# Sixteen small matrix products at a time instead of thirty-two interleaved, with index tables and one transpose moved

## The chip, the cores and the metric

The kernel runs on one core of one Trainium2 chip. The metric is the time of one execution on the device, in microseconds. TensorE (PE in the profile, with PEld for its weight loads) multiplies, VectorE (DVE), ScalarE (ACT) and GpSimd (POOL) work on elements, and SyncE (SP) starts loads. Each engine takes its own instructions in the order of the program and waits for the others by semaphores.

## The reference

Three layers follow each other. An attention layer with a gated recurrent state (4 batches, 8 heads, 768 steps, head size 40) makes 3072 rows of 320 numbers:

```python
for t in range(S):
    m_new = np.maximum(f_gate[:, :, t] + m, i_gate[:, :, t])
    f_stab = np.exp(f_gate[:, :, t] + m - m_new)
    i_stab = np.exp(i_gate[:, :, t] - m_new)
    C = f_stab[...] * C + i_stab[...] * np.einsum('bhd,bhe->bhde', vt, kt)
    n = f_stab[...] * n + i_stab[...] * kt
    denom = np.maximum(np.abs(np.einsum('bhd,bhd->bh', n, qt)), 1.0)
    y[:, :, t] = sigmoid(o_gate[:, :, t]) * np.einsum('bhde,bhe->bhd', C, qt) / denom
```

Then every row goes to one of 8 experts, 384 rows to each, in the order of the gate's logits over all rows (`x @ w_gate`, greedy by value), and through that expert's two matrices (`relu(x @ w1[e]) @ w2[e]`). Last, a dense layer: `elu(x @ w_in) @ w_out` with 2048 hidden units.

## The kernel before

The attention is cut in 12 chunks of 64 time steps. A step `u` (24 of them, `NU`) is one chunk of two batches and 8 heads. In a chunk the recurrence is written as matrix products of 64x64 blocks, in fp32. Two batches lie at partitions 0 to 63 and 64 to 127, so each kind of product comes as 16 matmuls: head `h` of 8, half `r` of 2. Every such matmul uses one quarter (64 rows by 64 columns) of TensorE's array, and the profile lists two records for it. The four kinds of step `u` are

- `values(u)`: the weighted scores `P` times the values `VP`, into the output `pO`;
- `scores(u + 2)`: keys times queries, two steps ahead, into `pS`;
- `recall(u)`: the faded queries `qt` times the state `CS`, added to the same `pO`;
- `state(u)`: the faded keys `kt` times the values, into `pC`.

The halves of `values` and `recall` use the two quarters on one diagonal of the array, those of `scores` and `state` the two on the other. `both(...)` issues, head by head, one pair of every kind that it is given.

`run` sets the order of a step on every engine, and nothing reorders it afterwards. TensorE: `values` with `scores`, `recall` with `state`, the transposes of the step before (`turn(u - 1)`), the rows of decay factors (`decay(u + 2)`), the logits of the step before (`logits(u - 1)`). VectorE: `scan` (a scan that makes `W`), `weigh` (`P`), then the denominators (`gates`: `rd`), the sum of the state (`add_state`) and the output `x` (`rows_out`). GpSimd: `factors(u + 1)` (`vp`, `qt`), the output gate `sg` times the reciprocal, then `fade(u + 1)` (`kt` and the state's fading). Between these stand pieces of later stages: `fill()` converts a weight matrix, and `step()` works through generators in `extra`, the router's tables and first comparisons among them. The tables (`Router.tables`) are index patterns written by GpSimd (iota and memset), with a few VectorE instructions after them; they are started by `hook(2)`, after step 2.

`sel` is a matrix of zeros and ones (96 by 2048, bf16) that `decay` multiplies by; VectorE builds it from the small `i3` at the start. `turn` transposes `x` in three blocks of 128 columns: `x` has 320 columns, and ScalarE copies columns 256 to 319 once more to 320 to 383. `logits` takes 128, 128 and 64 rows of the transposed blocks.

After the attention comes the routing of the first expert, then the experts and the dense layer, in an order that a planner writes out while the program is built.

Of the kernel before, what the change touches and what calls it, by code (L numbers as in the profile page):

```python
# [12 lines left out]
AF = mybir.ActivationFunctionType  # L13
# [4 lines left out]
NS, NU = 12, 24  # L18
# [16 lines left out]
class Plan:  # L35
# [3 lines left out]
    def __init__(self):  # L39
        self.n = 0  # L40
        self.todo = []
        self.reset()
# [39 lines left out]
    def next(self):  # L82
        self.due(min(self.todo)[0])
# [30 lines left out]
class Attention:  # L114
# [1 line left out]

    def __init__(self, nc, tc, consts, qk, vk, ig, fg, wg, xd, L, ident):
        self.nc, self.tc, self.qk, self.vk, self.xd, self.L, self.ident = nc, tc, qk, vk, xd, L, ident  # L120
        self.es = ExitStack()
        one = self.es.enter_context(tc.tile_pool(name="a1", bufs=1))
        self.two = self.es.enter_context(tc.tile_pool(name="a2", bufs=2))
        self.psX = self.es.enter_context(tc.tile_pool(name="psX", bufs=1, space=PS))
        V, G, A = nc.vector, nc.gpsimd, nc.scalar
        self.st = {}
        self.extra = []
        gi = one.tile([32, S], F32, name="gi")
        gf = one.tile([32, S], F32, name="gf")
        nc.sync.dma_start(gf, fg)  # L130
        A.dma_start(gi, ig)
        junk = self.psum("pF", 1)
        wz = one.tile([128, 512], BF, name="wz")
        V.memset(wz, 0.0)

        def spin(n):

            for _ in range(n):
                nc.tensor.matmul(junk, wz[:, :128], wz, start=True, stop=True)

        spin(SPIN)
        warm = one.tile([1, 8], F32, name="warm")
        V.memset(warm, 0.0)
        A.activation(warm, warm, AF.Exp)
        self.QKb = [one.tile([128, 2, 2, 8, 64], F32, name=f"qk{i}") for i in range(3)]
        self.QK, self.VK, self.W = {}, {}, {}
        for bp in range(2):
            self.load_qk(0, bp)
        self.load_vk(0)
        self.load_qk(1)  # L150
        self.wg = one.tile([128, 3, 8], F32, name="wg")
        nc.sync.dma_start(self.wg, wg)
        self.load_vk(1)
        self.VP = [one.tile([128, 8, 64], F32, name=f"vp{i}") for i in range(2)]
        m = one.tile([32, S + 1], F32, name="m")
        V.memset(m[:, 0:1], -1e30)
        d1 = one.tile([32, S], F32, name="d1")
        G.memset(d1, 0.0)
        for x in self.VP:
            G.memset(x[:, :, 41:], 0.0)  # L160
        i3 = one.tile([96, 32], BF, name="i3")
        for k in range(3):
            V.tensor_copy(i3[k * 32:k * 32 + 32], ident[:32, :32])
        self.sel = one.tile([96, 16, 2, 64], BF, name="sel")
        V.tensor_copy(self.sel, i3.rearrange("p (r m) -> p m r", r=2)[:, :, :, None].to_broadcast([96, 16, 2, 64]))
        self.id8 = one.tile([128, 8, 64], BF, name="id8")
        for r in (0, 64):
            A.activation(self.id8[r:r + 64], ident[r:r + 64, None, r:r + 64].to_broadcast([64, 8, 64]), AF.Copy)
        self.fp = one.tile([96, S], BF, name="fp")
        self.CS = [[one.tile([128, 8, 64], F32, name=f"C{b}{i}") for i in range(3)] for b in range(2)]  # L170
        for x in self.CS[0] + self.CS[1]:
            G.memset(x[:, :, 41:], 0.0)
        self.dp = one.tile([96, S], BF, name="dp")
        self.isT = one.tile([128, NS, 16], F32, name="isT")
        self.pC = self.psum("pC", 1)
        self.pG = self.psum("pX", 1).rearrange("p h t -> p (h t)")
        self.g = gi, gf, m, d1

        t0, t1 = slice(0, 128), slice(128, S)
        self.maximum(0, 128)  # L180
        V.tensor_tensor(gf[:, t0], gf[:, t0], m[:, t0], op=ALU.add)
        V.tensor_tensor(gf[:, t0], gf[:, t0], m[:, 1:129], op=ALU.subtract)
        V.tensor_copy(d1[:, 64:65], gf[:, 64:65])
        V.memset(gf[:, 0:128:64], 0.0)
        V.tensor_tensor(gi[:, t0], gi[:, t0], m[:, 1:129], op=ALU.subtract)
        g0 = gf[:, t0].rearrange("p (s t) -> p s t", t=64)[:, :, 1:]
        A.activation(g0, g0, AF.Exp)
        A.activation(self.fp[:32, t0], gf[:, t0], AF.Copy)
        A.activation(gi[:, t0], gi[:, t0], AF.Exp)
        self.maximum(128, 128 + MX[0])  # L190
        for k in (1, 2):
            V.tensor_tensor(m[:, t0], (gf if k == 1 else m)[:, t0], self.fp[k * 32 - 32:k * 32, t0], op=ALU.subtract)
            A.activation(self.fp[k * 32:k * 32 + 32, t0], m[:, t0], AF.Copy)
            self.maximum(128 + MX[k - 1], 128 + MX[k])
        A.activation(d1[:, 64:65], d1[:, 64:65], AF.Exp)
        self.both(self.scores(0))
        self.turn_gi(0, 2)
        self.decay(0)
        self.keep_gi(0, 2)
        V.memset(self.pC, 0.0)  # L200
        V.tensor_tensor(gf[:, t1], gf[:, t1], m[:, t1], op=ALU.add)
        self.scan(0)
        V.tensor_tensor(gf[:, t1], gf[:, t1], m[:, 129:], op=ALU.subtract)
        A.activation(gf[:, t1], gf[:, t1], AF.Exp)
        self.decay(1)
        self.both(self.scores(1))
        self.factors(0)
        self.weigh(0)
        self.fade(0)
        V.tensor_tensor(gi[:, t1], gi[:, t1], m[:, 129:], op=ALU.subtract)  # L210
        A.activation(gi[:, t1], gi[:, t1], AF.Exp)
        self.products(1, 2)
        for _ in self.parts(self.dp, d1, slice(64, 128)):
            pass
        self.opens(0)
# [217 lines left out]

    def turn(self, u):
        x = self.st.pop(("x", u))
        p = self.st["T", u] = self.psum("pX", 1).rearrange("p h t -> p (h t)")
        for k in range(3):
            self.nc.tensor.transpose(p[:, k * 128:k * 128 + 128], x[:, k * 128:k * 128 + 128], self.ident)
        xT = self.st["xT", u] = self.two.tile([128, 3, 128], F32, name="xT")
        self.nc.scalar.activation(xT.rearrange("p k t -> p (k t)"), p[:, :384], AF.Copy)  # L440

    def logits(self, u):

        l = self.st.pop(("T", u))[:, 384:392]
        x = self.st.pop(("xT", u))
        for k in range(3):
            z = 128 if k < 2 else 64
            self.nc.tensor.matmul(l, x[:z, k], self.wg[:z, k], start=k == 0, stop=k == 2)  # L448
        self.nc.scalar.activation(self.L[:, :, u % 4 * 6 + u // 4], l, AF.Copy)

    def step(self):
# [4 lines left out]
    def run(self, hook, fill):  # L456
        later = self.later()
        for u in range(NU):
            v, w = u + 1, u + 2
            fl = lambda i: ([fill() for _ in range(FP[i])] if u > FU else []) + [self.step() for _ in range(EP[i])]  # L460
            if u % 2 == 0 and u // 2 + 2 < NS:
                self.load_qk(u // 2 + 2)
                self.load_vk(u // 2 + 2)
            self.both(self.values(u), self.scores(w))
            self.both(self.recall(u), self.state(u))
            if u > 0:
                self.turn(u - 1)
            if v < NU:
# [32 lines left out]
class Router:  # L501
# [9 lines left out]
    def tables(self):  # L511
        nc, c, stage = self.nc, self.c, self.stage
        G, V = nc.gpsimd, nc.vector
# [21 lines left out]
        d = stage.tile([128, 128], F32, name="tri0", bufs=1)  # L535
# [8 lines left out]
        self.ax = c.tile([128, 24], F32, name="ax")  # L544
        self.thr0 = stage.tile([128, 128], I32, name="thr0", bufs=1)
        m = stage.tile([128, 128], I32, name="tblt", bufs=1)
        V.tensor_scalar(jt, jt, 25, None, op0=ALU.logical_shift_left)
        yield
        V.tensor_scalar(m, jt, 31, -1, op0=ALU.arith_shift_right, op1=ALU.bitwise_xor)
# [853 lines left out]
def kernel(ctx, tc, qk, vk, ig, fg, wg, w1a, w1b, w2a, win, wout, out):  # L1403
    nc = tc.nc
    consts = ctx.enter_context(tc.tile_pool(name="c", bufs=1))
# [8 lines left out]
    plan = Plan()  # L1414
    m = Mlp(nc, tc, consts, w1a, w1b, w2a, win, wout, xd, out, ident, rt, plan)
    stage = ctx.enter_context(ExitStack())
    sp = stage.enter_context(tc.tile_pool(name="cv", bufs=2))
    at = Attention(nc, tc, consts, qk, vk, ig, fg, wg, xd, L, ident)

    wp = m.win_pieces(sp)  # L1420

# [3 lines left out]
    def hook(u):  # L1425
        if u == FU:
            fill()
            fill()
        if u == 2:
            rt.__init__(nc, tc, consts, wk, L, sp, plan)  # L1430
            at.extra.append(rt.tables())
            at.step()
        if 4 <= u < 23 and u % 4 == 0:
            at.extra.append(rt.early(u // 4 - 1))
        if u == 22:
            at.extra.append(rt.early(5, 0, 2))
        if u == 23:
            at.extra.append(rt.early(5, 2, 3))
        if u == 24:
            while at.extra:  # L1440
                at.step()
            rt.dg = rt.digits(0)
            for _ in rt.early(5, 3, 4, rt.dg):
                pass
# [18 lines left out]
def _layout(i):  # L1463
# [19 lines left out]
    d["vk"] = np.concatenate([a.reshape(12, 128, 2, -1) for a in (v, by_token(i["k"]), by_token(i["o_gate"])[:, ::-1])], 3)  # L1483
    d["ig"], d["fg"] = (i[n].reshape(2, 2, 8, 768).swapaxes(0, 1).reshape(32, 768) for n in ("i_gate", "f_gate"))
    wg = i["moe_w_gate"][:, ::-1]
    d["wg"] = np.concatenate([wg, np.zeros((64, 8), wg.dtype)]).reshape(3, 128, 8).transpose(1, 0, 2)
    d["w1a"] = i["moe_w1"][:, :256].reshape(2048, 1024)
    d["w1b"] = i["moe_w1"][:, 256:].reshape(512, 1024)
    d["w2a"] = i["moe_w2"].reshape(8, 2, 4, 128, 320).transpose(0, 1, 3, 2, 4).reshape(2048, 1280)
# [20 lines left out]
```

## Time and profile before

| | us |
|---|---|
| median of 3 runs | 819.77 (814.91 to 820.18) |
| the profiled execution | 817.59 |
| its span | 815.8 |
| attention, start to the first routing matmul | 0 to 166.5 |
| of it steps 3 to 22, first `values` to first `values` | 36.48 to 157.09 |
| routing of the first expert and start of the experts | 166.6 to 200 |
| experts and dense layer | 200 to 815.8 |

The span is what the profiler saw between the first and the last instruction; 1.8 us of the execution's own time lie around it. The profile is of one execution, and its own time stands 2.2 us under the median.

### The profile page before, as it was taken

How to read it: one execution, taken by the hardware profiler on the slowest of the kernel's cores; microseconds unless marked ns; L12 is line 12 of the kernel's file. 1: busy time of each engine (PE TensorE's matmuls, PEld its weight loads, DVE VectorE, ACT ScalarE, POOL GpSimd, SP SyncE). 2: the span in 40 equal slices, each digit the busy share in tenths (PEclk: the TensorE clock that was granted, in tenths of full speed). 3: DMA queues.
4: the chain of work that ended last, by engine and by line, in shares of the span. 5: the costliest groups of instructions: out<-in, count | busy, mean ns of one | idle time of the engine just before them, and what ended most of it. 6: DMA issues, size and time to landing. Idle time of an engine off the chain costs nothing.

```text
span 815.8 us, 18330 instructions
## 1 busy us (share of the span) xinstructions
PE 729.8 (89%) x7355; PEld 681.9 (84%) x7355; DVE 586.1 (72%) x1616; ACT 348.5 (43%) x743; POOL 309.2 (38%) x358
## 2 busy tenths in 40 slices
PE   7788788836899799799999999999999999999995
PEld 5678678725788789789989988898999999999995
DVE  8697878777979976987897679867733942862542
ACT  5343334324356533543553255325533633742431
POOL 3687887626425631633134125213410601201001
PEclk8678787856999999999999999999999999999998
DMA  8766855135114202112123103200500410100000
GB/s 343 253 216 209 278 186 187 43 107 199 54 30 139 83 27 78 51 44 100 32 65 93 40 0 106 67 27 0 172 12 13 138 35 25 65 1 26 1 1 25
DMA packets 20757, 72.79 MB, mean 89 GB/s; under 512 B 3200, under 2 KB 7296, under 8 KB 19264
## 3 DMA queue, kind: packets, MB, share of 16 engines
q1 hardware_dynamic: 8336, 35.08, 12.6%
q0 software_dynamic: 8448, 31.73, 11.8%
q10 hardware_dynamic: 3888, 4.82, 2.1%
q8 instruction: 58, 0.95, 0.5%
q14 instruction: 27, 0.22, 0.1%
HBM read 62.96 MB, written 8.65 MB: 88 GB/s over the span
## 4 chain that ended last, share of the span: by engine, by line
PE 58%; DVE 21%; issue 8%; ACT 4%; DMA 4%; POOL 2%; ACTq 1%; SPq 0%; POOLq 0%; DVEq 0%
PE ph L1096 24%; PE acc L1234 5%; PE acc L1238 4%; PE acc L1235 4%; PE acc L1203 3%; PE acc L1205 3%; PE acc L1204 3%; DVE e L1149 2%; DMA xd<-x 2%; PE pr L727 2%; DVE ge L713 1%; DVE gl L980 1%; PE acc L1190 1%; PE pX L448 1%; DMA vk<-in_vk_dram 1%
## 5 line engine op out<-in xcount | busy, mean ns | idle before, releaser
L1234 PE MATMUL acc<-woh,gh 128*128 128x320 f32 x384 | 122.7, 320 | 0.0
L1238 PE MATMUL acc<-woh,gl 128*128 128x320 f32 x384 | 119.7, 312 | 0.0
L1235 PE MATMUL acc<-wol,gh 128*128 128x320 f32 x384 | 119.0, 310 | 0.0
L1149 DVE SCALAR_TENSOR_TENSOR e<-e,ph 128x384 f32<-128x384 f32 x128 | 69.9, 549 | 61.8 <-ACT e L1146 61.4
L1145 ACT ACTIVATE e<-ph 128x384 f32<-128x384 f32 x128 | 62.7, 489 | 116.3 <-PE ph L1096 112.0
L980 POOL TENSOR_TENSOR gl<-e,gh 128x384 fp32r<-128x384 f32 x33 | 34.8, 1057 | 164.3 <-DVE gh L974 132.3
L1096 PE MATMUL ph<-yh,wih 128*128 128x384 f32 x256 | 89.7, 351 | 0.4
L1096 PE MATMUL ph<-yh,wil 128*128 128x384 f32 x256 | 86.2, 337 | 0.0
L1113 ACT ACTIVATE gh<-ph 128x384 fp32r<-128x384 f32 x64 | 31.3, 491 | 121.9 <-PE ph L1096 120.7
L1244 POOL DMA_INDIRECT out_dram<-ot,idx x24 | 24.0, 1001 | 141.3 <-ACT ot L972 138.1
L1120 DVE SCALAR_TENSOR_TENSOR gl<-ph,gh 128x384 fp32r<-128x384 f32 x64 | 35.4, 556 | 56.8 <-ACT gh L1113 56.4
L1238 PEld LDWEIGHTS acc<-woh,gl 128*128 128x128 f32 x384 | 72.5, 189 | 0.6
L1234 PEld LDWEIGHTS acc<-woh,gh 128*128 128x128 f32 x384 | 72.8, 190 | 0.2
L1235 PEld LDWEIGHTS acc<-wol,gh 128*128 128x128 f32 x384 | 72.7, 189 | 0.0
L1146 ACT ACTIVATE e<-e 128x384 f32<-128x384 f32 x128 | 67.3, 526 | 4.0
L1096 PE MATMUL ph<-yl,wih 128*128 128x384 f32 x256 | 66.5, 341 | 0.0
L980 DVE TENSOR_TENSOR gl<-e,gh 128x384 fp32r<-128x384 f32 x95 | 57.3, 607 | 1.9
L1096 PEld LDWEIGHTS ph<-yh,wih 128*128 128x128 f32 x256 | 48.4, 189 | 4.5 <-ACT yh L1208 4.4
L1096 PEld LDWEIGHTS ph<-yh,wil 128*128 128x128 f32 x256 | 48.3, 189 | 0.0
L1096 PEld LDWEIGHTS ph<-yl,wih 128*128 128x128 f32 x256 | 46.4, 189 | 0.0
L1096 PE MATMUL ph<-xh,w1h 128*128 128x384 f32 x128 | 45.0, 352 | 0.2
L1203 PE MATMUL acc<-gh,w 128*128 128x384 f32 x128 | 44.6, 349 | 0.0
(269 smaller groups left out, 2023.5 us busy)
## 6 DMA issues: line engine op xcount, KB each, us to landing
vk<-in_vk_dram SPq DMA_DIRECT2D x12, 968.0 KB, 8.7
qk<-in_qk_dram SPq DMA_DIRECT2D x11, 1024.0 KB, 8.0
wx<-in_wout_dram SPq DMA_DIRECT2D x16, 320.0 KB, 2.8
xd<-x ACTq DMA_DIRECT2D x48, 96.0 KB, 3.7
cx<-in_win_dram SPq DMA_DIRECT2D x8, 512.0 KB, 4.4
qk<-in_qk_dram SPq DMA_DIRECT2D x2, 512.0 KB, 5.9
cx<-in_win_dram SPq DMA_DIRECT2D x4, 256.0 KB, 4.2
xg<-xd,idx POOLq DMA_INDIRECT x24, 3.3
```

The source lines that it names most:

```text
L980: (self.nc.vector if e == "d" else self.nc.gpsimd).tensor_tensor(out, x, y, op=ALU.subtract)
L1096: PE.matmul(p, w, x, start=k == 0, stop=k == 7)
L1113: nc.scalar.activation(h, p, AF.Relu)
L1120: nc.vector.scalar_tensor_tensor(l, p, 0.0, h, op0=ALU.max, op1=ALU.subtract)
L1145: nc.scalar.activation(e, p, AF.Relu, scale=-1.0)
L1146: nc.scalar.activation(e, e, AF.Exp, scale=-1.0)
L1149: nc.vector.scalar_tensor_tensor(e, e, -1.0, p, op0=ALU.add, op1=ALU.max)
L1203: PE.matmul(p, w[:, c], h, start=f == 0, stop=False)
L1204: PE.matmul(p, w[:, cl], h, start=False, stop=False)
L1234: PE.matmul(p, h[:, c], self.woh[:, f], start=f == 0, stop=False)
L1235: PE.matmul(p, h[:, c], self.wol[:, f], start=False, stop=False)
L1238: PE.matmul(p, l[:, c], self.woh[:, f], start=False, stop=f == 15)
```

## The change

Five edits. `run` calls `both` once for each kind, so that TensorE gets 16 matmuls of one kind, then 16 of the next. The router is made ahead of the attention, and the part of `tables` on GpSimd is issued in the attention's start; its VectorE part stays behind step 2. `i3` is made by ScalarE and `sel` by GpSimd instead of VectorE. The third transpose takes columns 192 to 319, so that `turn` no longer reads the copied columns (the copy and the store of 384 columns stay), and `logits` takes rows 64 to 127 of that block, with `wg` laid out to match. The last step's `turn` writes to a buffer of `pS` instead of `pX`.

```diff
@@ Attention.__init__
         for k in range(3):
-            V.tensor_copy(i3[k * 32:k * 32 + 32], ident[:32, :32])
+            A.activation(i3[k * 32:k * 32 + 32], ident[:32, :32], AF.Copy)
         self.sel = one.tile([96, 16, 2, 64], BF, name="sel")
-        V.tensor_copy(self.sel, i3.rearrange("p (r m) -> p m r", r=2)[:, :, :, None].to_broadcast([96, 16, 2, 64]))
+        G.tensor_copy(self.sel, i3.rearrange("p (r m) -> p m r", r=2)[:, :, :, None].to_broadcast([96, 16, 2, 64]))
...
         for x in self.CS[0] + self.CS[1]:
             G.memset(x[:, :, 41:], 0.0)
+        next(tables)
@@ turn
-        p = self.st["T", u] = self.psum("pX", 1).rearrange("p h t -> p (h t)")
+        p = self.st["T", u] = self.psum(*(("pX", 1) if u < NU - 1 else ("pS", 2))).rearrange("p h t -> p (h t)")
         for k in range(3):
-            self.nc.tensor.transpose(p[:, k * 128:k * 128 + 128], x[:, k * 128:k * 128 + 128], self.ident)
+            c = min(k * 128, 192)
+            self.nc.tensor.transpose(p[:, k * 128:k * 128 + 128], x[:, c:c + 128], self.ident)
@@ logits
-            z = 128 if k < 2 else 64
-            self.nc.tensor.matmul(l, x[:z, k], self.wg[:z, k], start=k == 0, stop=k == 2)
+            z = 0 if k < 2 else 64
+            self.nc.tensor.matmul(l, x[z:, k], self.wg[z:, k], start=k == 0, stop=k == 2)
@@ run
-            self.both(self.values(u), self.scores(w))
-            self.both(self.recall(u), self.state(u))
+            self.both(self.values(u))
+            self.both(self.scores(w))
+            self.both(self.recall(u))
+            self.both(self.state(u))
@@ tables: after the GpSimd part
         m = stage.tile([128, 128], I32, name="tblt", bufs=1)
+        yield
         V.tensor_scalar(jt, jt, 25, None, op0=ALU.logical_shift_left)
@@ tile_mlstm_moe_mlp_kernel
-    at = Attention(nc, tc, consts, qk, vk, ig, fg, wg, xd, L, ident)
+    rt.__init__(nc, tc, consts, wk, L, sp, plan)
+    tables = rt.tables()
+    at = Attention(nc, tc, consts, qk, vk, ig, fg, wg, xd, L, ident, tables)
...
         if u == 2:
-            rt.__init__(nc, tc, consts, wk, L, sp, plan)
-            at.extra.append(rt.tables())
+            at.extra.append(tables)
             at.step()
```

TensorE, step 8 of the attention, from the logits of the step before to the transposes, before (`pO<-vp,P` is `values`, `pS` `scores`, `pO<-C,qt` `recall`, `pC` `state`, `pX<-ident,x` the transposes):

```order
L448 MATMUL pX<-wg,xT 128x8 x3
L368 MATMUL pO<-vp_121,P 64x64 x2
L283 MATMUL pS<-qk_111 64x64 x2
...
L382 MATMUL pO<-C_140,qt 64x64 x2
L394 MATMUL pC<-vp_121,kt 40x64 x2
...
L438 MATMUL pX<-ident,x 128x128 x3
```

The same place now:

```order
L450 MATMUL pX<-wg,xT 128x8 x3
L369 MATMUL pO<-vp_121,P 64x64 x16
L284 MATMUL pS<-qk_111 64x64 x16
L383 MATMUL pO<-C_140,qt 64x64 x16
L395 MATMUL pC<-vp_121,kt 40x64 x16
L440 MATMUL pX<-ident,x 128x128 x3
```

Before, a pair of one kind and a pair of the other took turns 8 times; now each kind stands in one piece, and all of `recall` stands ahead of the first matmul of `state`.

GpSimd, from its first memsets to the first `vp` and on through the tables, before:

```order
L160 MEMSET vp_122 128x8x23
L172 MEMSET C_139 128x8x23
...
L316 TENSOR_TENSOR vp_121<-vk,isT 128x8x41
L328 TENSOR_TENSOR kt<-vk,W 128x320
...
L330 TENSOR_TENSOR C_144<-C_143,db 128x8x41
L517 IOTA pc 64x1 x2
...
L543 MEMSET one_628 128x48
L316 TENSOR_TENSOR vp_121<-vk,isT 128x8x41
```

GpSimd's start now:

```order
L160 MEMSET vp_122 128x8x23
L165 COPY sel<-i_129 96x2048
L172 MEMSET C_139 128x8x23
...
L521 IOTA pc 64x1 x2
...
L547 MEMSET one_177 128x48
L317 TENSOR_TENSOR vp_121<-vk,isT 128x8x41
L329 TENSOR_TENSOR kt<-vk,W 128x320
```

The copy that makes `sel` and all 17 iotas and memsets of the tables moved ahead of the first `vp`. From the end of the attention on, every engine's order is what it was.

## Rows read from the trace of the kernel before

**Rows 1.** The page: the span, and the engine's busy time.

```profile
span 815.8 us, 18330 instructions
PE 729.8 (89%) x7355; PEld 681.9 (84%) x7355; DVE 586.1 (72%) x1616; ACT 348.5 (43%) x743; POOL 309.2 (38%) x358
```

**Rows 2.** Windows: PE, PEld, DVE, ACT, POOL busy us, granted clock, DMA share, GB/s.

```profile
36.48:157.09 120.61, 100.82 (x2982) 93.00 (x2981) 102.18 (x209) 46.86 (x121) 98.31 (x112) 0.79 0.59 194
152.70:158.00 5.30, 4.28 (x104) 3.93 (x105) 4.33 (x11) 1.48 (x5) 3.66 (x4) 1.00 0.18 42
158.10:166.60 8.50, 6.72 (x58) 5.63 (x53) 2.96 (x15) 1.58 (x5) 0.85 (x1) 0.50 0.19 46
200.00:815.80 615.80, 582.90 (x3669) 551.66 (x3669) 425.76 (x1229) 270.95 (x555) 177.20 (x190) 0.99 0.16 53
```

**Rows 3.** Timeline of TensorE from one step to the next: start us, us, engine, line.

```profile
76.50 0.55 PE L438 MATMUL pX<-ident,x 128*128 128x128 f32 x3
...
78.48 0.27 PE L368 MATMUL pO<-vp,P 64*64 64x64 f32 x2
78.50 0.27 PE L283 MATMUL pS<-qk 64*64 64x64 f32 x2
...
79.47 0.28 PE L382 MATMUL pO<-C,qt 64*64 64x64 f32 x4
```

**Rows 4.** Timeline of TensorE in steps 22 and 23, without `scores` and `state`.

```profile
152.65 1.15 PE L368 MATMUL pO<-vp,P 64*64 64x64 f32 x32
153.63 1.10 PE L382 MATMUL pO<-C,qt 64*64 64x64 f32 x32
154.66 0.55 PE L438 MATMUL pX<-ident,x 128*128 128x128 f32 x3
156.23 0.93 PE L448 MATMUL pX<-wg,xT 128*128 128x8 f32 x6 [1.02 <-ACT xT L440]
157.09 1.20 PE L368 MATMUL pO<-vp,P 64*64 64x64 f32 x32
158.07 1.93 PE L382 MATMUL pO<-C,qt 64*64 64x64 f32 x32
...
163.23 0.90 PE L438 MATMUL pX<-ident,x 128*128 128x128 f32 x3 [0.28 <-ACT L L449]
```

**Rows 5.** Waits of TensorE, 36 to 157 us: us in total, times, longest.

```profile
PE pC L394 <- POOL kt L328: 5.2, 6, 1.7
PE pO L382 <- issue: 4.8, 3, 2.4
...
PE pC L394 <- issue: 1.8, 2, 1.2
PE pD L291 <- issue: 1.7, 2, 1.0
PE pX L448 <- issue: 1.3, 1, 1.3
```

**Rows 6.** Timeline of VectorE and GpSimd at the start, and of the tables.

```profile
1.36 2.09 DVE L163 CAST i<-ident 32x32 bf16<-32x32 f32 x3 [0.18 <-POOL ident masks.py:199]
3.48 1.24 DVE L165 COPY sel<-i 96x2048 bf16<-96x2048 bf16 x1
4.64 0.46 DVE L224 TENSOR_TENSOR_SCAN m<-gf,m,gi 32x128 f32<-32x128 f32 x1
11.59 0.74 POOL L316 TENSOR_TENSOR vp<-vk,isT 128x328 f32<-128x328 f32 x1 [7.96 <-DMA vk<-in_vk_dram]
34.45 0.32 POOL L517 IOTA pc<- 64x1 f32 x2
35.51 0.75 POOL L526 IOTA kx<- 128x192 bf16 x1
37.84 0.13 POOL L543 MEMSET one<- 128x48 f32 x1
```

More of the change, by code (lines that the diff above doesn't have):

```diff
@@ L114, with __init__ @@
 class Attention:
-    def __init__(self, nc, tc, consts, qk, vk, ig, fg, wg, xd, L, ident):
+    def __init__(self, nc, tc, consts, qk, vk, ig, fg, wg, xd, L, ident, tables):
         self.nc, self.tc, self.qk, self.vk, self.xd, self.L, self.ident = nc, tc, qk, vk, xd, L, ident
@@ L1485, in _layout @@
     wg = i["moe_w_gate"][:, ::-1]
-    d["wg"] = np.concatenate([wg, np.zeros((64, 8), wg.dtype)]).reshape(3, 128, 8).transpose(1, 0, 2)
+    d["wg"] = np.concatenate([wg[:256], np.zeros((64, 8), wg.dtype), wg[256:]]).reshape(3, 128, 8).transpose(1, 0, 2)
     d["w1a"] = i["moe_w1"][:, :256].reshape(2048, 1024)
```

## Prediction

> **What bounds the kernel now.** I read the page first: TensorE is busy for 729.8 of 815.8 us, VectorE for 586.1 [rows 1]. The windows by stage say that this is two different things. From 200 us on TensorE is busy for 582.90 of 615.80 us at a granted clock of 0.99 [rows 2]; there it is the bound, and the change doesn't touch that stage. The change lies in the attention. Steps 3 to 22 take 120.61 us, that is 6.03 us a step; TensorE is busy for 100.82 of them, VectorE for 102.18, GpSimd for 98.31, and the granted clock is 0.79 [rows 2]. [...]
>
> So I read TensorE's own timeline at the upper level. From the transposes to the next step's `values` it takes 78.48 - 76.50 = 1.98 us (transposes, decay rows, logits and the wait for the copy between them), and `values` with `scores`, interleaved, 79.47 - 78.48 = 0.99 us [rows 3]. With another 0.99 for `recall` with `state`, a step that never waits at the upper level would take 3.96 us. The other 2.07 us of the 6.03 are idle time, (120.61 - 100.82) / 20 = 0.99, and some 1.1 that the lower level costs. The list of waits says what the idle time is: 5.2 us for `kt` from GpSimd, and 4.8 + 1.8 + 1.7 + 1.3 = 9.6 us marked "issue", in which nothing that the profile shows was awaited [rows 5].
>
> **The pairs.** Steps 22 and 23 have no `scores` and no `state`, so the trace already shows pairs of one kind by themselves. At the upper level `values` alone takes 153.63 - 152.65 = 0.98 us and `recall` alone 154.66 - 153.63 = 1.03 us [rows 4]: as long as twice the number of products interleaved. The four quarters of the array do run at once before, and after the change two of them stand empty at any moment. The change therefore adds 2 x 0.98 - 0.99 = 0.97 us to each group. There are 22 groups with `scores` and 20 with both `recall` and `state`: 42 x 0.97 = 41 us more work for TensorE at the upper level, and twice that at the lower one, where `recall` alone lasts 1.93 instead of 1.10 us [rows 4].
>
> That is work, not yet time, because TensorE has those 2.07 us a step to spare. A step is then 3 x 0.98 + 1.03 + 1.98 = 5.95 us. At the three joins between kinds the neighbours use different quarters, so the first pair of a kind can start beside the last of the one before, which is worth up to 0.06 a join (0.99 / 16); with part of that I take 5.85 us. VectorE needs 102.18 / 20 = 5.1 and GpSimd 4.9 us a step [rows 2], so TensorE becomes the engine that sets the step, by a little: 20 x 5.85 = 117 us against 120.61, if it never waited and never fell to the lower level.
>
> What it would still wait for. The 5.2 us for `kt` go: `recall` was tied to `state` pair by pair and so waited for `kt` too, while now it runs ahead, the denominators start a little after it, and `state` comes 2.9 us after `values` instead of 1. I cost that wait at nothing; the cover is the 0.98 of `scores` and the 1.03 of `recall`, and if GpSimd falls behind by more than that the wait returns at `state`, with the transposes, decay rows and logits queued behind it. The "issue" waits I can't derive. Three of the longest lie inside interleaved products; if they are a supply that short bursts run dry, pieces twice as long dry it less, and if not, they now lie on an engine that sets the time. Bounds 0 and 9.6 us; I take half, 4.8.
>
> The clock. In rows, the level was 1.00 from 152.70 to 158.00, where the products were pairs of one kind, and 0.50 from 158.10 on [rows 2]; before it fell TensorE had waited 1.02 us for `xT` [rows 4]. So pairs alone held the level for two steps, and an idle stretch came before the fall. A TensorE that is occupied for nearly the whole step should stay up for most of the time. [...] I take two spells of some 3.5 us after the longest "issue" waits (2.4 us), in which half is lost: 3.5 us. The sum of the loop is 117 + 4.8 + 3.5 = 125.3, or +4.7 us.
>
> **The start.** Taking `i3` and `sel` from VectorE frees 4.72 - 1.36 = 3.4 us ahead of its first scan [rows 6]. But the first `values` needs `vp` as well, and `vp` begins at 11.59, when a load lands that the change doesn't move. What GpSimd takes over has to fit into the 7.96 us that it was idle before that `vp` [rows 6]: the tables, 37.97 - 34.45 = 3.5 us, and `sel`. No row has `sel` on GpSimd; bounds are VectorE's 1.24 us and the iota's price of 0.75 us for 192 columns, 8.0 us for 2048; by `vp`, 0.74 for 328 columns and the nearest in kind, it is 4.6 us. 3.5 + 4.6 = 8.1: it just fits, or delays the first `vp` by some tenths. [...] No row of this trace decides it, and the sum differs by less than 1 us.
>
> The tables held GpSimd for those 3.5 us after step 2, and the next `vp` stood behind them. They now lie in the idle start. That is worth 0 to 3.5 us; TensorE's step 3 began at 36.48 [rows 2], while they ran, and with the added products TensorE comes to `values` of step 4 later still, so I take 0. For the start as a whole I take 0, with -4 and +5 as bounds.
>
> **The end.** The last transposes waited 0.28 us for the logits' copy, which shares `pX` [rows 4]; with `pS` that goes. The copy of 64 columns is still made, only the transposes no longer read it. -0.3 us; up to -3 if the last two steps stay at the upper level, where the transposes took 0.55 instead of 0.90 and `recall` 1.10 instead of 1.93.
>
> **The sum.** +4.7 + 0 - 0.3 = +4.4 us: 817.59 becomes 822.0 by the profiled execution, and 824.2 beside the median of 819.77, which stands 2.2 above it. I predict 824. What a measurement of this kernel can tell from no change is about 1%, 8.2 us.
>
> **Rivals.** First, the spare time isn't there: every "issue" wait stays (9.6 instead of 4.8), and after each of the six or so longer waits TensorE falls to the lower level, 20 us at half the rate instead of 7 (10 instead of 3.5). That is +16 us, 836, with a range of 829 to 840. For it speaks that TensorE has no slack left to hide a wait; against it, that the denser work of 152.70 to 158.00 held the level through a wait of a microsecond for a while. It decides from about 8 us of such losses more than I took.
>
> Second, pairs don't bring the level back up once it is down, since half of the array is empty. At the lower level a step costs 4 x 1.9 for the kinds and about 3 us for the rest (0.90 against 0.55 for the transposes), 10.6 instead of 5.85. If a third of the 20 steps run so, that is 7 x 4.75 = +33 us, 855; with all of them +95. For it: the `recall` of step 23, alone at 1.93 us, was not followed by a rise; 158.10 to 166.60 stays at 0.50 [rows 2]. Against it: that stretch was idle for a fifth of its time, and the loop's would not be.
>
> Third, the level holds all along and the "issue" waits hide: 117 - 120.6 - 0.3 = -3.9, with the start and the end at their better values -8 to -10, so 810 to 816. [...]
>
> **Chances.** My forecast 0.55, the first rival 0.22, the second 0.12, the third 0.11. Faster than 1% needs the third with its end at its best: 0.06. Slower than 1% (828) is the first and the second and a little of the forecast's own upper end: 0.36. Within 1%: 0.58. The forecast's own range is 816 to 829; for 8 in 10 it has to reach into the first and the third rival and leaves the second out: 814 to 840.
>
> **What would show it.** In the profile after, TensorE's `values`, `scores`, `recall` and `state` should each take 0.95 to 1.05 us at the upper level; steps 3 to 22 should last 117 to 130 us with TensorE busy for over 90% and a granted clock above 0.9; waits for `kt` under 2 us; the first `vp` still near 11.6 us. A clock under 0.8 there, or a first `vp` after 14 us, would prove me wrong, as would a step shorter than 5.7 us.

## The result, and the profile after

The changed kernel takes 822.34 us (median of 16 runs, 819.92 to 827.77) beside 817.99 us for the kernel before (16 runs, 812.23 to 824.89) on the same chip. The ratio is 1.0055, with a 95% interval of 1.0034 to 1.0077: slower by half a per cent, with an interval clear of 1, and within the 1% that the prediction called no change. The profiled execution took 821.81 us.

The page of the changed kernel: span, busy time of the engines, and one of the DMA queues (packets, MB, share of 16 engines).

```profile
span 820.0 us, 18331 instructions
...
PE 744.3 (91%) x7355; PEld 698.5 (85%) x7355; DVE 581.9 (71%) x1612; ACT 348.9 (43%) x746; POOL 311.8 (38%) x359
...
q8 instruction: 58, 0.95, 0.5%
```

Three windows of it: steps 3 to 22 ("the loop"), the last step up to the first routing matmul, and the rest. Columns as in [rows 2].

```profile
36.84:160.81 123.97, 112.43 (x2981) 106.41 (x2980) 98.83 (x208) 46.51 (x121) 96.47 (x103) 0.92 0.58 187
160.81:168.55 7.74, 5.51 (x83) 4.81 (x83) 3.13 (x16) 1.76 (x6) 0.85 (x1) 0.86 0.22 54
168.55:820.00 651.45, 598.92 (x3768) 564.63 (x3767) 451.99 (x1336) 283.02 (x580) 192.74 (x206) 0.96 0.18 58
```

The loop lasts 123.97 us where [rows 2] have 120.61. TensorE is busy for 112.43 of them instead of 100.82, and the granted clock has risen from 0.79 to 0.92. So TensorE does more work at a higher clock, and the stage has become 3.4 us longer all the same. What it waits for in the loop (columns as in [rows 5]):

```profile
PE pC L395 <- issue: 4.5, 2, 2.3
PE pD L292 <- issue: 1.9, 1, 1.9
PE pS L284 <- issue: 1.3, 1, 1.3
PE pO L383 <- issue: 1.3, 2, 0.9
PE pX L450 <- ACT xT L442: 0.8, 2, 0.6
```

The wait for `kt`, 5.2 us in [rows 5], is gone. The "issue" waits are nearly all still there: 4.5 + 1.9 + 1.3 + 1.3 = 9.0 us, against 10.2 before: the 9.6 of [rows 5] and one row more.

```profile
PE pS L283 <- issue: 0.6, 1, 0.6
```

TensorE's timeline of one step at the upper level (a granted clock of 1.00; at the lower one it is 0.50, as in [rows 2]), from `values` to the next `values` (the rows in which two kinds overlap are left out):

```profile
43.54 0.97 PE L369 MATMUL pO<-vp,P 64*64 64x64 f32 x26
44.30 0.27 PE L284 MATMUL pS<-qk 64*64 64x64 f32 x2
...
45.06 0.27 PE L383 MATMUL pO<-C,qt 64*64 64x64 f32 x2
...
45.82 0.25 PE L395 MATMUL pC<-vp,kt 64*40 64x64 f32 x2
...
46.84 0.55 PE L440 MATMUL pX<-ident,x 128*128 128x128 f32 x3
...
48.83 0.97 PE L369 MATMUL pO<-vp,P 64*64 64x64 f32 x26
```

From the start of one kind to the start of the next it is 0.76 us, three times (44.30 - 43.54, 45.06 - 44.30, 45.82 - 45.06). Only `state`, with the transposes behind it, takes 1.02. The first row shows how: it ends after 26 of its 32 records, because the last three matmuls of `values` (two records each) run beside the first of `scores`. A step lasts 48.83 - 43.54 = 5.29 us.

At the start, GpSimd and VectorE:

```profile
3.82 1.71 DVE L225 TENSOR_TENSOR_SCAN m<-gf,m,gi 32x128 f32<-32x128 f32 x1 [2.64 <-DMA gi<-in_ig_dram]
3.38 1.88 POOL L165 COPY sel<-i 96x2048 bf16<-96x2048 bf16 x1 [1.00 <-ACT i L163]
11.43 1.27 POOL L317 TENSOR_TENSOR vp<-vk,isT 128x328 f32<-128x328 f32 x1 [1.60 <-DMA vk<-in_vk_dram]
```

The first scan begins 0.8 us earlier than in [rows 6] and waits for a load; it then takes 1.71 us instead of 0.46 and so ends later. `sel` takes 1.88 us on GpSimd. The first `vp` starts at 11.43 (11.59 before) and still waits for `vk`.

At the end, the last transposes and logits:

```profile
165.12 0.55 PE L440 MATMUL pS<-ident,x 128*128 128x128 f32 x3 [0.24 <-DVE x L428]
167.08 1.54 PE L450 MATMUL pS<-wg,xT 128*128 128x8 f32 x6 [1.41 <-ACT xT L442]
```

The wait for the logits' copy [rows 4] is gone; a wait of 0.24 us for `x` itself stands in its place. The transposes take 0.55 instead of 0.90 us, since the upper level now lasts until here (granted clock 1.00 from 160.81 to 166.30; in [rows 2] 0.50 from 158.10 on): 7.74 us from the last `values` to the first routing matmul, where before it was 166.53 - 157.09 = 9.44.

### The profile page after: what moved, and what is told of

Its sections match the earlier page's. It is cut to its first block, busy times and chain, and to the rows that moved or that the text cites. A ratio compares the mean times of both kernels' runs of the same rounds, so it can differ in the third digit from the quotient of the medians.

```text
span 820.0 us, 18331 instructions
## 1 busy us (share of the span) xinstructions
PE 744.3 (91%) x7355; PEld 698.5 (85%) x7355; DVE 581.9 (71%) x1612; ACT 348.9 (43%) x746; POOL 311.8 (38%) x359
## 3 DMA queue, kind: packets, MB, share of 16 engines
q1 hardware_dynamic: 8336, 35.08, 12.6%
## 4 chain that ended last, share of the span: by engine, by line
PE 52%; DVE 16%; issue 6%; ACT 3%; DMA 1%; POOL 1%; POOLq 0%; ACTq 0%; DVEq 0%
PE ph L1101 24%; PE acc L1239 5%; PE acc L1243 4%; PE acc L1240 4%; PE acc L1208 3%; PE acc L1210 3%; PE acc L1209 3%; DVE e L1154 2%; PE pr L732 2%; DVE gl L985 1%; PE acc L1195 1%; DVE ge L718 1%; PE acc L1197 1%; ACT e L1150 1%; ACT e L1151 1%
```

## The experiments

All were timed beside the kernel before on the same chip: e1 to e4 together, then e5 to e8, e9 with e10, and e11 with e12. "Loop" runs from the first `values` of step 3 to that of step 23 in the profile of each; "rest" begins at the first routing matmul.

| run | ratio (95%) | loop us | clock | issue us | kt us | rest us |
|---|---|---|---|---|---|---|
| before | 1 | 120.6 | 0.79 | 10.2 | 5.2 | 649.3 |
| changed | 1.0055 (1.0034 to 1.0077) | 124.0 | 0.92 | 9.0 | 0 | 651.5 |
| e1_pairs_only | 1.0054 (1.0033 to 1.0075) | 127.5 | 0.91 | 10.3 | 0 | 656.6 |
| e2_rest_only | 1.0019 (0.9995 to 1.0044) | 122.6 | 0.78 | 14.6 | 3.7 | 654.3 |
| e3_split_recall | 1.0019 (0.9995 to 1.0042) | 121.4 | 0.91 | 14.0 | 1.0 | 654.7 |
| e4_filler | 1.0110 (1.0073 to 1.0147) | 126.6 | 0.85 | 11.6 | 1.0 | 655.6 |
| e5_after_no_loads | 0.9900 (0.9868 to 0.9932) | 115.7 | 0.97 | 0 | 3.2 | 651.7 |
| e6_before_no_loads | 0.9897 (0.9853 to 0.9941) | 114.3 | 0.83 | 3.0 | 10.6 | 651.9 |
| e7_kind_order | 1.0086 (1.0057 to 1.0115) | 128.5 | 0.96 | 10.9 | 0 | 650.9 |
| e8_spread_loads | 1.0018 (0.9984 to 1.0053) | 122.6 | 0.96 | 10.8 | 0 | 650.2 |
| e9_small_packets | 1.0050 (1.0027 to 1.0074) | 123.9 | 0.94 | 11.1 | 0 | 650.3 |
| e10_skip_zero_rows | 1.0036 (1.0010 to 1.0062) | 125.9 | 0.92 | 11.3 | 0 | 648.9 |
| e11_before_lean_loads | 0.9918 (0.9890 to 0.9947) | 117.5 | 0.84 | 11.9 | 4.3 | 655.8 |
| e12_after_again | 1.0077 (1.0048 to 1.0106) | 127.5 | 0.91 | 11.0 | 0 | 656.1 |

Each row is one profile. Two profiles of the same changed kernel (the second and the last row) differ by 3.5 us in the loop and by 4.6 in the rest, so differences of that size between single rows say nothing; the ratios are of 4 to 16 runs each.

### Which part of the change carries the effect

**e1_pairs_only** is the kernel before with the four calls in `run` alone; **e2_rest_only** is the changed kernel with the two interleaved calls put back.

```diff
-            self.both(self.values(u), self.scores(w))
-            self.both(self.recall(u), self.state(u))
+            self.both(self.values(u))
+            self.both(self.scores(w))
+            self.both(self.recall(u))
+            self.both(self.state(u))
```

> The kernel before with one edit: each kind of small product issued by itself, as after the change; the tables, sel, i3 and the transposes stay as before. My theory: the pairs make the loop what it is after the change, TensorE-paced at a high clock, and the other four edits are worth less than 2 us together. Then steps 3 to 22 take 121 to 127 us (after 123.97, before 120.61), the granted clock there is 0.88 to 0.95, and the ratio to before is 1.003 to 1.010. Rival: the added time comes from the start (VectorE's first scan and the first vp came 0.4 us later) or from chance beyond the attention, and the pairs are neutral: ratio 0.998 to 1.002.

> The changed kernel with values and scores, and recall and state, interleaved again as before; early tables, sel on GpSimd, i3 on ScalarE and the moved transposes stay. My theory: these edits are worth 0 to -2 us (a later start by 0.4 us, the wait of the last transposes gone, the tables out of step 3), ratio 0.997 to 1.000, loop 117 to 122 us at a clock of 0.75 to 0.85. Rival: they cost time (sel and the tables crowd GpSimd's start), ratio 1.002 or more.

The pairs alone give 1.0054, the whole of the 1.0055; the other four edits together give 1.0019, which isn't told apart from no change and lies between the range of its theory (up to 1.000) and that of the rival (from 1.002). e1's loop is half a microsecond longer than expected. The start, the tables and the end may be left out of the search.

### Decoupling without the work, and work without the pairs

**e3_split_recall** keeps `values` with `scores` interleaved and separates only `recall` from `state`: half of the added work, and the whole of the decoupling from `kt`. **e4_filler** is the kernel before with 12 small bf16 matmuls a step into unused columns of `pX`, ahead of the logits; nothing reads their result.

```diff
@@ e3, in the changed kernel
-            self.both(self.values(u))
-            self.both(self.scores(w))
+            self.both(self.values(u), self.scores(w))
@@ e4, in the kernel before
+    def filler(self, u, n):
+        for _ in range(n):
+            self.nc.tensor.matmul(self.st["T", u][:, 392:512], self.wz[:, :128], self.wz[:, :120], start=True, stop=True)
...
+                self.filler(u - 1, 12)
                 self.logits(u - 1)
```

> The changed kernel with values and scores interleaved again, recall and state each by itself. Half of TensorE's added work is gone, but recall still doesn't wait for kt. If untying recall from state is what the change gained, and the 41 us of added work what it cost, the loop keeps the gain at half the cost: a step at the upper level is 0.99 + 0.76 + 1.02 + 1.99 = 4.8 us, VectorE's 5.1 us set the step, 20 steps with 9 us of issue waits partly hidden take 110 to 118 us, ratio 0.988 to 0.997. Rival: what the change gained is the clock, from TensorE being occupied throughout; with less work it falls more often (0.80 to 0.87) and the loop takes 118 to 123 us, ratio 0.997 to 1.003.

> The kernel before, with 12 additional matmuls a step whose results nobody reads (128x120, bf16, zeros, into unused columns of pX, just ahead of the logits). They add 12 x 0.05 = 0.6 us of TensorE a step at the upper level and change no dependence of the real work. If the lower level is what costs the loop before its 1.1 us a step, the clock rises from 0.79 to 0.88 or more and the loop takes 108 to 116 us, ratio 0.985 to 0.995. Rival: the waits set the step and the clock is only their trace: the clock may rise, but the loop takes 119 to 124 us, ratio 0.998 to 1.005.

Both theories missed. In e3 the upper-level step is 4.7 us, the clock is 0.91 and the wait for `kt` 1.0 us, and yet the time is that of the kernel before: the "issue" waits are 14.0 us. Ratio and loop are those of its rival, but the rival's clock of 0.80 to 0.87 is not. In e4 the clock rose as well, to 0.85, and the kernel became 1.1% slower, outside both ranges. The 0.05 us of one of its matmuls was an estimate, and the trace of before gives the same: bf16 matmuls of 128x512 at its start begin 0.216 us apart at a granted clock of 1.00 (4.53 to 5.18 us), 0.05 for 120 columns. The loop of e4 has 239 matmuls more, and TensorE is busy for 108.08 us of it instead of 100.82. With more work on TensorE the granted clock rose, from 0.79 to 0.85 in e4 and 0.92 in the changed kernel; the time did not fall. Here the clock was bought with added work, and the "issue" waits stayed.

### What the "issue" waits are

Four of the changed kernel's waits in its timeline, the idle time in brackets:

```profile
31.22 0.97 PE L395 MATMUL pC<-vp,kt 64*40 64x64 f32 x26 [1.34 <-issue]
59.49 0.31 PE L395 MATMUL pC<-vp,kt 64*40 64x64 f32 x4 [2.12 <-issue]
86.62 0.22 PE L292 MATMUL pD<-dp,sel 96*128 96x64 bf16 x2 [1.94 <-issue]
124.39 0.58 PE L395 MATMUL pC<-vp,kt 64*40 64x64 f32 x13 [2.35 <-issue]
```

They stand in the middle of a kind, at `state` of steps 2, 6 and 16 and at the last decay row of step 10. The page's instruction queue q8 has 58 packets of 0.95 / 58 MB, some 16 KB each. In windows of 0.25 us a packet of q8 begins at 28.75, 57.25, 84.00 and 122.00: each of the four waits ends 2.2 to 2.6 us after the start of one of these windows. The DMA queues in the window at 57.25 us (packets, MB, share of 16 engines):

```profile
q1 hardware_dynamic: 13, 0.08, 73.9%
q8 instruction: 1, 0.02, 24.1%
```

And windows of all engines, of the last of the four waits and of a stretch behind it:

```profile
122.04:124.39 2.35, 0.00 (x1) 0.00 (x1) 1.61 (x5) 0.00 (x0) 2.35 (x2) 1.00 0.95 349
125.50:132.20 6.70, 6.70 (x130) 6.65 (x128) 3.19 (x5) 2.95 (x7) 3.26 (x4) 0.50 0.93 324
```

During that wait the DMA engines are 95% busy, with the loads on q1. This wait costs twice: behind it TensorE stands at the lower level (0.50) for 6.7 us. In the whole span the page counts 7355 matmuls, 7355 weight loads and the 58 packets of q8: some 254 of these instructions to a packet.

So the theory was that TensorE's own instructions arrive late when the loads of `qk` and `vk` fill the DMA engines; the rival, that the waits belong to those instructions. **e5_after_no_loads** and **e6_before_no_loads** leave the loads for chunks 3 to 11 out, in the changed kernel and in the one before; those chunks are computed from the data of chunks 0 to 2 again.

```diff
-            if u % 2 == 0 and u // 2 + 2 < NS:
-                self.load_qk(u // 2 + 2)
-                self.load_vk(u // 2 + 2)
+            n = u // 2 + 2
+            if u == 0:
+                self.load_qk(n)
+                self.load_vk(n)
+            elif u % 2 == 0 and n < NS:
+                self.QK[n], self.VK[n] = self.QK[n - 3], self.VK[n - 3]
```

> The changed kernel, but the loads of keys, queries and values for chunks 3 to 11 are left out: those chunks use the tiles of chunks 0 to 2 again, so the outputs are those of other inputs. Theory A (the waits of TensorE marked issue are its own instructions arriving late: each of them ended 1 to 2.5 us into a packet of the instruction queue, at times at which the load queue filled the 16 DMA engines): the issue waits of steps 3 to 22 fall from 9.0 us to under 2, the clock there rises from 0.92 to over 0.97, and the loop takes 107 to 111 us instead of 124; ratio to the kernel before 0.985 to 0.993. Theory B (the waits belong to the instructions at those places whatever the loads do): 8 to 10 us of issue waits stay, the loop stays within 2 us of 124 and the ratio is 1.002 to 1.008.

> The kernel before, with the same loads left out. Theory A: issue waits under 2 us instead of 9.6, and the loop 106 to 113 us instead of 120.6, held there by VectorE (102 us busy) and by the waits for kt; the difference to the changed kernel without loads is then under 3 us, since TensorE's added work of 26 us (20 steps, 5.29 instead of 3.96 us) lies beside VectorE's. Theory B: issue waits of 8 to 10 us and a loop of 118 to 122 us.

The window of the loop in e5:

```profile
34.36:150.02 115.66, 107.45 (x2982) 100.84 (x2981) 100.36 (x208) 46.35 (x122) 97.78 (x103) 0.97 0.28 74
```

Its waits of TensorE there, all of them:

```profile
PE pC L395 <- POOL kt L329: 3.2, 4, 1.2
PE pX L450 <- ACT xT L442: 1.9, 5, 0.6
PE pF L292 <- DVE W L310: 1.2, 2, 0.6
```

The same window of e6:

```profile
35.04:149.35 114.31, 97.34 (x2981) 89.47 (x2980) 103.72 (x209) 46.78 (x121) 99.59 (x111) 0.83 0.28 75
```

And the longest of its waits:

```profile
PE pC L394 <- POOL kt L328: 10.6, 8, 1.9
PE pX L448 <- ACT xT L440: 1.5, 5, 0.6
PE pC L394 <- issue: 1.3, 2, 1.0
PE pX L448 <- issue: 1.0, 1, 1.0
PE pO L382 <- issue: 0.7, 2, 0.5
```

In e5 not one "issue" wait is left, the clock is 0.97, and the time falls by 1.5% of the changed kernel's. In e6 10.2 us become 3.0. The rival is out. And without the loads the two kernels are equal, 0.9900 and 0.9897 (medians of 810.42 and 809.99 us): the added TensorE work (20 steps of 5.29 instead of 3.96 us) then costs nothing that can be measured. What e5 spends on it, e6 spends waiting for `kt` (10.6 us) and at the lower level (0.83). The half per cent is there only with the loads. The sizes of the loops missed by 1 to 5 us: in e5 waits for `kt`, `xT` and `W` of 6.3 us came up from underneath, and in e6 3.0 us of "issue" are more than the 2 expected.

### The joins between the kinds

**e7_kind_order** swaps two calls, so that neighbours use the same quarters of the array at two of the three joins.

```diff
             self.both(self.values(u))
-            self.both(self.scores(w))
             self.both(self.recall(u))
+            self.both(self.scores(w))
             self.both(self.state(u))
```

> The changed kernel with the kinds in the order values, recall, scores, state: values and recall use the same two quarters of the array, scores and state the other two, so only one of the three joins inside a step lies between different quarters. Theory A (the 0.76 us of a kind instead of the 0.98 that I predicted is overlap of the last pairs of one kind with the first of the next, possible only between different quarters): values and scores take 0.98 to 1.03 us each, recall still 0.76 to 0.8, the step at the upper level 5.6 to 5.8 us instead of 5.29, and the loop 3 to 9 us longer than that of the changed kernel; ratio to the kernel before 1.008 to 1.016. Theory B (a kind of 16 takes 0.76 us whatever stands beside it): the step stays at 5.29 and the ratio at 1.003 to 1.008.

The same step in its timeline:

```profile
44.04 1.15 PE L369 MATMUL pO<-vp,P 64*64 64x64 f32 x32
45.02 0.92 PE L383 MATMUL pO<-C,qt 64*64 64x64 f32 x26
45.74 0.27 PE L284 MATMUL pS<-qk 64*64 64x64 f32 x2
...
46.72 1.06 PE L395 MATMUL pC<-vp,kt 64*40 64x64 f32 x32
47.71 0.55 PE L440 MATMUL pX<-ident,x 128*128 128x128 f32 x3
...
49.69 0.51 PE L369 MATMUL pO<-vp,P 64*64 64x64 f32 x10
```

`values`, with `recall` behind it on the same quarters, lasts 0.98 us and is one row of 32 records; `recall`, with `scores` behind it on the others, 0.72; `scores` again 0.98. The step is 49.69 - 44.04 = 5.65 us, in the range expected; the loop is 4.5 us longer than the changed kernel's in the first profile and 1.0 longer than in the second, and the ratio 1.0086 instead of 1.0055, with intervals that still overlap. It is the step that shows it: the last matmuls of a kind run beside the first of the next where the quarters differ, and not where they are the same.

### Other loads

**e8_spread_loads** loads half of a chunk at every step; **e9_small_packets** puts a gap into the tiles, so that the pieces are 2 and 3.9 KB instead of 8 and 7.7; **e10_skip_zero_rows** loads only the 40 rows of 64 that aren't zero, 19% fewer bytes. All three are edits of the changed kernel.

```diff
@@ e8 (load_vk takes bp in the same way)
-            if u % 2 == 0 and u // 2 + 2 < NS:
-                self.load_qk(u // 2 + 2)
-                self.load_vk(u // 2 + 2)
+            if u // 2 + 2 < NS:
+                bp = slice(u % 2, u % 2 + 1)
+                self.load_qk(u // 2 + 2, bp)
+                self.load_vk(u // 2 + 2, bp)
@@ e9
-        self.QKb = [one.tile([128, 2, 2, 8, 64], F32, name=f"qk{i}") for i in range(3)]
+        self.QKb = [one.tile([128, 2, 2, 9, 64], F32, name=f"qk{i}")[:, :, :, :8] for i in range(3)]
@@ e10
-        self.nc.sync.dma_start(self.QK[n][:, bp], self.qk[n, :, bp])
+        for p in [slice(0, 128)] if n < 3 else [slice(0, 40), slice(64, 104)]:
+            self.nc.sync.dma_start(self.QK[n][p, bp], self.qk[n, p, bp])
```

> The changed kernel with each load of keys and queries and of values cut in its two halves, one half of both at every step instead of both whole at every second step. If an instruction packet is late because of the depth of the load queue at that moment, the issue waits fall from 9.0 to 3 to 6 us and the time by 3 to 8 us, ratio 0.995 to 1.002. If it is late whenever any load is under way, the waits stay at 7 to 11 us, since the loads take as long in total, and the ratio stays at 1.002 to 1.008.

> The changed kernel with a gap in the tiles of keys and queries and of values, so that a load comes in pieces of 2 and 3.9 KB instead of 8 and 7.7 KB; the same bytes at the same times. If TensorE's instructions are late because their packets take turns with the load's packets on the same DMA engines, shorter pieces let them through sooner: issue waits of steps 3 to 22 of 4 to 7 us instead of 9.0, loop 118 to 122, ratio to the kernel before 0.997 to 1.003. If it is the share of the bytes that counts, the issue waits stay at 8 to 11 us and the ratio at 1.002 to 1.008.

> The changed kernel, in which the loads of keys and queries for chunks 3 to 11 take only the 40 rows of each 64 that are not zero (the zeros lie in the three tiles since the first loads): 640 instead of 1024 KB for each, which is 19% less for both loads together. Without any of these loads the issue waits went from 9.0 to 0 and the time fell by 1.5% of the changed kernel's; in proportion to the bytes 19% less gives 1.7 us of the waits and 2.3 us of the time, ratio to the kernel before 0.998 to 1.004. If only a full queue matters and the waits depend on where a packet falls, they may change by more or not at all: 5 to 11 us.

None of them took the waits away: 10.8, 11.1 and 11.3 us. So no one of these three, the depth of the queue, the size of its pieces or a fifth of its bytes, is what the waits hang on, as far as one profile of each can tell. The ratio of e8, 1.0018, is better than its waits: its loop begins at 34.71 instead of 36.84 us. e10's begins at 33.72.

**e11_before_lean_loads** is the kernel before with the edits of e8 and e10 together, **e12_after_again** the changed kernel unaltered, for a second profile.

> The kernel before (interleaved products) with both edits of the loads: halves at every step, and without the zero rows from chunk 3 on. Without the loads the kernel before gained 1.0% and its issue waits fell from 9.6 to 3.0 us. If the waits follow the bytes, a fifth of that is to be had: ratio 0.996 to 0.999, and the version is as fast as or a little faster than both kernels. If only a full queue counts, as the last two runs say for the changed kernel, the issue waits stay at 8 to 12 us and the ratio is 0.998 to 1.002, save for an earlier start (loop beginning 2 to 3 us sooner), which would give 0.996 to 0.998.

> The changed kernel once more, for a second profile. If the loop carries the difference to the kernel before, it lasts 122 to 126 us again with issue waits of 8 to 11 us, at the same instructions as in the first profile (state in step 2 and late in step 6, the decay rows of step 10, state in step 16), and the time from the first routing matmul on differs from the first profile's 651.5 by as much as from the kernel before's 649.3. If the experts carry it, that time is above 651 again. Ratio 1.003 to 1.008.

e11 is the fastest that computes the whole: 816.92 us (12 runs), ratio 0.9918, and 1.5% under the changed kernel on the same chip (829.50). That is a larger gain than any of the ranges expected. The window of its loop:

```profile
32.81:150.31 117.50, 97.61 (x2981) 89.31 (x2981) 101.02 (x209) 47.03 (x122) 101.89 (x122) 0.84 0.63 184
```

Its longest waits of TensorE there:

```profile
PE pC L396 <- POOL kt L330: 4.3, 7, 1.1
PE pO L384 <- issue: 4.2, 4, 2.0
PE pD L293 <- issue: 3.4, 2, 2.1
```

The loop begins 3.7 us earlier than in [rows 2], at 32.81: between 14 and 38 us the kernel before waits 2.4 us for "issue" and 1.7 for `isT`, and this one 0.8 and nothing. The loop itself is 3.1 us shorter, no more than two profiles of one kernel differ, and 11.9 us of "issue" waits remain in it; the clock is 0.84 instead of 0.79. Which of the two edits does what isn't told apart, nor why the clock held better.

In e12's timeline the same instructions wait as in the changed kernel's first profile:

```profile
31.16 1.71 PE L395 MATMUL pC<-vp,kt 64*40 64x64 f32 x26 [3.19 <-issue]
60.76 0.31 PE L395 MATMUL pC<-vp,kt 64*40 64x64 f32 x4 [2.39 <-issue]
87.28 0.22 PE L292 MATMUL pD<-dp,sel 96*128 96x64 bf16 x2 [1.39 <-issue]
127.48 0.96 PE L395 MATMUL pC<-vp,kt 64*40 64x64 f32 x13 [3.72 <-issue]
```

Same place, other lengths. The loop is 127.5 us, above the 122 to 126 that I expected.

What the place is, the traces can tell. Three windows of the changed kernel's first profile, each from the end of one "issue" wait to the end of another:

```profile
31.21:59.48 28.27, 24.09 (x634) 22.75 (x634) 20.13 (x43) 10.09 (x25) 18.98 (x21) 0.88 0.56 190
86.61:97.81 11.20, 10.15 (x254) 9.77 (x254) 9.62 (x18) 3.91 (x10) 10.67 (x12) 0.85 0.85 280
97.81:103.18 5.37, 4.93 (x127) 4.53 (x126) 4.46 (x9) 2.06 (x6) 4.17 (x6) 1.00 0.93 282
```

Matmuls and weight loads together are 1268, 508 and 253, that is 5, 2 and 1 times some 254. With TensorE's few other instructions, which the windows leave out, the trace has 1280, 512 and 256, to within one. All 95 "issue" waits over 0.2 us that the fourteen profiles have between 36 and 160 us stand, to within one instruction, at the same place in a count by 256: where one block of 256 instructions ends and the next begins. Each block has its packet of q8. Counted block by block, the 95 waits end 2.2 to 2.9 us after the start of that packet (one 3.8), and no block, with a wait or without, begins sooner than 2.2 us after it. A packet takes 0.9 to 2.1 us in every profile. What the loads move is its start: in the changed kernel it lies 1.6 us (median) behind the beginning of the block before, and in e5 0.6. So these waits are late instructions.

A load isn't the only way to be late. In e6 a packet starts at 51.92 us, 1.2 us after the block before was begun and behind a microsecond in which the DMA engines moved nothing; the wait that ends at 54.40 still lasts 1.0 us, because the interleaved products used up that block in 2.65 us. In e5 no block of the loop is used up in less than 3.6 us, and no wait is left.

## Why the prediction was right, and where it was not

The forecast was +4.4 us by profiled executions; they stand 4.2 apart, and the ratio of all runs makes it +4.5. The mechanism that it named is the one that the runs show: pairs make TensorE the engine with the least to spare, the wait for `kt` goes, and the "issue" waits, which it couldn't explain, stay and now lie on it. e5 and e6 show it best, since without the loads the kernels tie. The other signs that it named came too: TensorE busy for 91% of the loop, a clock above 0.9, a first `vp` at 11.43 us. But that the sum came out is luck, because errors cancelled: the steps were taken 12.5 us too long, the "issue" waits and the lower level together 10.6 too short.

| term | predicted us | profile after us |
|---|---|---|
| steps 3 to 22 at the upper level | 117 | 104.5 (19 x 5.29, and 3.99 for step 22, which has no `scores` and no `state`) |
| wait for `kt` | 0 | 0 |
| "issue" waits | 4.8 | 9.0 |
| lower level | 3.5 | 9.9 (0.08 x 123.97) |
| waits for `xT` in the loop | in the step | 0.2 (0.6 more lie in the 3.99) |
| loop | 125.3 | 123.6 summed, 123.97 measured |
| start | 0 | +0.4 |
| end | -0.3 | -1.7 |
| rest | 0 | +2.2 |

- **The step.** "Worth up to 0.06 a join" was wrong. I took the time of one matmul of a kind (0.99 / 16) at each join; three of the sixteen run beside the next kind, and a join is worth 0.98 - 0.76 = 0.22 us, as e7 shows by taking two of the joins away. The prediction said that a step shorter than 5.7 us would prove it wrong, and 5.29 did: this term, not the total. Step 22, which has neither `scores` nor `state`, was counted as a whole step besides.
- **The "issue" waits.** I took half of them for want of a reason. They are late instructions, and the change takes none of their cause away; the upper bound of 9.6 (10.2 with the row that [rows 5] leave out) was the value to take. The reason was to be had from the trace of before, whose waits stand at ends of blocks of 256 instructions as well, the five of over 1 us beside loads, with the DMA engines 82 to 98% busy.
- **The clock.** Two spells of 3.5 us were expected in the loop; its first 3 us and three spells, each behind one of the four long waits shown above, make 9.9 us of loss. Behind the other waits, of 0.3 to 1.3 us, it didn't fall (1.00 from 91.35 to 125.40). These two terms are the first rival's (10 us of waits, 10 of lower level), and its price of +16 us would have come true with the step that I had taken.
- **The second rival**, that pairs don't bring the level back, is out: TensorE returns to 1.00 within the loop each time (in the windows 40.10 to 60.50, 67.45 to 87.80, 91.35 to 125.40 and 132.30 to 160.81). (Its 855 us start from the profiled execution, the first rival's 836 from the median.) **The third**, that the level holds and the waits hide, is out as well, by the 9.9 and the 9.0 us.
- **The start.** `sel` took 1.88 us, not the 4.6 that I took by the row for `vp`. Nothing hung on it. The first scan became slower where GpSimd now works beside it; that this is why, and that it gave the 0.4 us, isn't shown. e1, which leaves the start as it was, begins its loop at 38.28 us, and the changed kernel at 36.84 in one profile and 37.87 in the other.
- **The end.** The wait that the change removes was replaced by one for `x`, so the -0.3 isn't there; the -1.7 is the upper level, which I had put into the bound of -3.
- **The rest.** From the first routing matmul on, every engine's order is the same in all fourteen profiles, and the time runs from 648.9 to 656.6 us; two profiles of the same changed kernel have 651.5 and 656.1, and e11, with interleaved products but on the same chip as the second, 655.8. The +2.2 between the first two profiles therefore says nothing about the change, and without it they are 2.0 us apart, not 4.2.

How the 4.5 us of the ratio divide between the loop and the end of the attention can't be read from one profile of a kernel: the changed kernel's own loop is 124.0 in one and 127.5 in the other.

## What to carry to other kernels

Idle time marked "issue" on a busy engine is to be set against the instruction queue and the DMA load at that moment, before a change is costed: here TensorE, whose instructions came late, gained nothing from being decoupled from GpSimd (the 5.2 us for `kt` went, the ratio is 1.0055), and the four longest of those waits cost again in clock behind them (0.50 to 0.53 for 3.2 to 6.7 us). A raised clock is no gain by itself; e4 and the change itself raised it (from 0.79 to 0.85 and 0.92) and lost time (1.0110 and 1.0055). Added work on an engine isn't free because the engine has idle time: here it cost nothing without the loads (0.9900 beside 0.9897) and half a per cent with them.

## What the runs showed of the hardware that was not expected

- Two kinds of 16 products of 64x64, one behind the other, overlapped by three products where they used different quarters of the array (0.72 us a kind in e7 and 0.76 in the changed kernel), and not at all where they used the same (0.98 in e7).
- For every 256 of TensorE's instructions there was a packet of q8, which the page counts on the same 16 DMA engines as the loads on q1 (0.5% and 12.6% of the span), and a block of 256 began no sooner than 2.2 us after the start of its packet. That packet started 1.6 us (median) behind the beginning of the block before with the loads, and 0.6 without them. With the loads, six waits of 0.3 to 2.4 us in the loop of the changed kernel; without them none. Loads of half the size, pieces of a quarter to a half, and 19% fewer bytes left the waits (10.8 to 11.3 us).
- The longest waits fall on the same instructions in both profiles of the changed kernel, at ends of such blocks, 1.3 to 2.4 us in one and 1.4 to 3.7 us in the other.
